# Moving two input loads from ScalarE's queue to SyncE's, so that the function table loads behind three loads, in a fused attention and rational-MLP kernel

## The chip, the cores and the metric

One core of one Trainium2 chip. The metric is device time in microseconds of one execution; most executions of one kernel here lie within 1 us of their median. Smaller is better. The span in a profile is about 1.8 us shorter than the device time of the same run.

## The reference

```python
def _attn_ref(q, k, v):                       # 8 batches, 12 heads, 448 rows, 64 columns
    scores = (1 / sqrt(64)) * q @ k^T
    m = max(scores); e = exp(scores - m)
    return (e / (sum(e) + exp(-m) + 1e-9)) @ v

def _moe_ref(x, w_in, w_out, a, b):           # x: 3584 x 768, w_in: 768 x 2048
    h = x @ w_in
    P = a[0] + a[1]*h + a[2]*h^2 + a[3]*h^3
    Q = 1 + |b[0]|*|h| + |b[1]|*h^2
    return (P / (Q + 1e-6)) @ w_out
```

The attention output, heads side by side, is x of the second part.

## The kernel before

The kernel is emitted by a small planner: operations are put into queues with estimated durations and latencies, the planner simulates the engines, and the instructions are emitted in the order it finds. Heads go in "quads" of four. For quads 0 and 1 of batch 0, float32 pieces are loaded on SyncE and ScalarE and cast to float16 by VectorE (one piece by ScalarE). Every v, and k and q from quad 2 on, are loaded by GpSimd and cast in the transfer. TensorE transposes k and q of quads 0 to 5; the head concerns 0 to 2. The exponentials are counted in the order in which ScalarE runs them; each needs its pass of scores.

```python
def first_loads():
    ...
    plan.add("c0", piece(0, 0, 0, 2, "ACT", 2.8))          # k, heads 0-1, first half
    plan.add("c0", piece(1, 0, 0, 2, "SP", 2.65))          # q, heads 0-1
    plan.add("c0", piece(0, 0, 2, 2, "ACT", 3.0, "ACT"))   # k, heads 0-1: cast by ScalarE
    piece(1, 1, 0, 2, "SP", 3.0)
    piece(0, 1, 0, 2, "ACT", 3.4)                          # k, heads 2-3
    piece(0, 1, 2, 2, "SP", 3.4)
    for pr in range(2):                                    # quad 1: k on ScalarE, q on SyncE
        for ti, (src, dst, dma) in enumerate(((k, kn, "ACT"), (q, qn, "SP"))):
            stage = quad1_stage(ti, pr)
            d = load(dma, src, 4 + 2 * pr, 2, stage, 0, J, 4.3 + 1.1 * pr)
            cast(1, ti, pr, 0, J, dst[1][:, 2 * pr:2 * pr + 2], stage, d)
    ...

# TensorE's order in the head: t* transposes (a-c, l: quad 0, d-e: quad 1, f-g: quad 2),
# s* score passes, A* sums over the exponentials and products with v
START = ("ta tb s0 tc s1 s2 td s3 s4 te s5 tf s6 s7 s9 s8 tg A0 "
         "s10 tl s11 A1 ...")

# in the main body, after first_loads():
table = plan.add("head", Op("table", "ACT", 1.3, [], lambda:
    nc.scalar.preload_act_table_set("natural_log_exp_and_others")))
...
vz = plan.add("cpt", Op("vz", "DVE", 0.06, [first_casts[0, 1, 0, 0]],
                        lambda: nc.vector.memset(vn[0][:, 0, 0, 0:2], 0.0)))
loads(0, "v")                 # GpSimd's first load; the memset before it holds it back
vload[0].deps.append(vz)
loads(2, "kq")                # quad 2
```

In the profiles, L397 is a load of `first_loads`, L402/L403 the casts, L471 the transposes, L557 the score passes, L566 the exponentials, L600 the sums and the products with v, L666 and L764 the two matrix products of the second part, L823 the function table.

The softmax here doesn't subtract the row's maximum and nothing guards it: scores larger than these inputs give would overflow.

## Time and profile before

| | kernel before |
|---|---|
| device time, median of the first 3 runs | 432.22 us (431.87 to 432.61) |
| span of the profiled run | 429.1 us (its device time 430.86 us) |
| table load | 3.74 to 5.02 us |
| first / second / seventh exponential starts | 6.43 / 8.00 / 13.46 us |
| q of quad 2 has landed | 12.69 us |
| first matmul with w_in | 27.77 us |

The profiled run was a good 1 us faster than the timed ones, so small differences of one trace to another must be held against the timed runs. The prediction below shows the lines. A line of a timeline is start, duration, engine, source line, operation, tiles, count, and in brackets the idle time before it and what ended it. A line of waits is: who waited, for whom, us in total, times, longest.

### The profile page before, as it was taken

To read this page: it belongs to the slowest core of one execution; us is meant where nothing else is said; L and a number is where in the kernel's file an instruction comes from. 1 tells how busy PE (TensorE), PEld (TensorE's weight loads), DVE (VectorE), ACT (ScalarE), POOL (GpSimd) and SP (SyncE) were. 2 spreads that over 40 slices of the span, in tenths; PEclk is the share of its full clock that TensorE was granted. 3 is DMA by queue.
4 is the path that set the end of the run, shared out by engine and by line. 5 is a ranking of instruction groups with operands and counts; after the bars stand their busy time and mean duration, and the time that the engine had idled before them with its cause. 6 is when DMAs were issued, how large, how long until landed. Compare 5 with 4: busy or idle time off the path is not lost.

```text
span 429.1 us, 8895 instructions
## 1 busy us (share of the span) xinstructions
PE 416.8 (97%) x3680; PEld 220.5 (51%) x3680; DVE 344.5 (80%) x513; ACT 328.6 (77%) x419; POOL 119.4 (28%) x170
## 2 busy tenths in 40 slices
PE   5899999999999999999999999999999999999996
PEld 3566665444444445444445544445444455555663
DVE  5344999989998869797999998789887699989500
ACT  4798999998989884988877489996788844875421
POOL 6456344365108233460013710333000000000000
PEclk9699999999999999999999999999999999999999
DMA  9999999997516994295143990296210111111222
GB/s 196 200 202 204 181 185 190 165 164 108 103 38 85 183 132 121 31 143 98 22 101 81 158 132 23 43 145 83 59 37 2 38 37 38 37 39 33 78 72 76
DMA packets 78185, 43.58 MB, mean 102 GB/s; under 512 B 36160, under 2 KB 74560, under 8 KB 78144
## 3 DMA queue, kind: packets, MB, share of 16 engines
q0 software_dynamic: 36928, 21.89, 37.5%
q1 hardware_dynamic: 39952, 20.26, 23.9%
q10 hardware_dynamic: 1264, 0.85, 0.8%
q8 instruction: 29, 0.48, 0.5%
q14 instruction: 12, 0.10, 0.1%
HBM read 45.62 MB, written 11.01 MB: 132 GB/s over the span
## 4 chain that ended last, share of the span: by engine, by line
PE 89%; DVE 5%; DMA 2%; ACT 2%; issue 1%; POOL 0%
PE gen L764 33%; PE gen L666 32%; PE gen L600 13%; PE sps L557 8%; DMA qn<-in_q_dram 2%; ACT e L566 2%; PE gen L557 1%; DVE h L683 1%; DVE n L703 1%; PE gen L471 1%; DVE n L707 1%; DMA h<-in_k_dram 1%; DVE g L707 0%; DVE c L707 0%; DVE c L703 0%
## 5 line engine op out<-in xcount | busy, mean ns | idle before, releaser
L566 ACT ACTIVATE e<-sps 112x896 f16<-112x896 f32 x156 | 137.8, 922 | 31.6 <-PE sps L557 30.9
L666 PE MATMUL gen<-x,w_in 128*128 128x448 f16 (+1 forms) x864 | 160.3, 332 | 0.0
L764 PE MATMUL gen<-w_out,g 128*128 128x384 f16 (+2 forms) x768 | 134.6, 326 | 0.7 <-DVE h L683 0.7
L666 PEld LDWEIGHTS <-w_in 128*128 128x128 f16 x864 | 80.2, 98 | 69.5 <-issue 15.7
L764 PEld LDWEIGHTS <-g 128*128 128x128 f16 x768 | 73.0, 98 | 58.6 <-issue 10.9
L683 DVE CAST h<-gen 128x448 f16<-128x448 f32 x113 | 69.3, 618 | 21.6 <-PE gen L666 17.6
L707 DVE TENSOR_TENSOR n<-n,h 128x1792 f16<-128x1792 f16 x64 | 70.2, 1096 | 1.0
L786 ACT ACTIVATE o<-gen 128x384 f32<-128x384 f32 (+2 forms) x56 | 27.9, 498 | 47.6 <-PE gen L764 46.7
L718 ACT ACTIVATE c<-c,oneeps_c 128x1792 f16<-128x1792 f16 x32 | 57.7, 1802 | 5.6 <-DVE c L707 5.5
L741 POOL COPY gx<-g 128x1024 f16<-128x1024 f16 x8 | 9.1, 1140 | 168.1 <-DVE g L707 120.5
L721 ACT ACTIVATE c<-c 128x1792 f16<-128x1792 f16 x32 | 54.8, 1713 | 0.2
L557 PE MATMUL sps<-qt,kt 64*128 64x448 f16 (+1 forms) x360 | 48.8, 341 | 2.0 <-ACT e L566 1.5
L703 DVE TENSOR_SCALAR n<-n,abc 128x1792 f16<-128x1792 f16 x64 | 44.7, 699 | 1.4
L600 PE MATMUL gen<-e,vn 112*32 112x448 f16 (+1 forms) x864 | 41.8, 337 | 0.0
L516 POOL COPY kp<-kn 112x256 uint32<-112x256 uint32 x36 | 23.0, 669 | 62.7 <-DMA kt<-kp 42.1
L628 DVE TENSOR_TENSOR x<-gen,lden 128x448 f16<-128x448 f32 (+1 forms) x54 | 28.3, 565 | 13.4 <-ACT lden L616 13.2
L707 DVE TENSOR_TENSOR g<-n,c 128x1792 f16<-128x1792 f16 x32 | 34.9, 1091 | 3.2 <-ACT c L721 2.5
L571 ACT ACTIVATE e<-gen 112x448 f16<-112x448 f32 x72 | 35.6, 560 | 0.0
L707 DVE TENSOR_TENSOR c<-c,w 128x1792 f16<-128x1792 f16 x32 | 35.0, 1092 | 0.2
L516 POOL COPY qp<-qn 112x256 uint32<-112x256 uint32 x36 | 26.9, 775 | 23.8 <-DMA qt<-qp 23.0
L557 PEld LDWEIGHTS <-kt 64*128 64x128 f16 x432 | 15.8, 96 | 32.1 <-issue 26.5
L600 PEld LDWEIGHTS <-vn 112*32 112x32 f16 x864 | 23.2, 99 | 14.1
(47 smaller groups left out, 288.9 us busy)
## 6 DMA issues: line engine op xcount, KB each, us to landing
vn<-in_v_dram POOLq DMA_DIRECT2D x24, 224.0 KB, 7.4
kn<-in_k_dram POOLq DMA_DIRECT2D x22, 224.0 KB, 7.4
qn<-in_q_dram POOLq DMA_DIRECT2D x22, 224.0 KB, 8.0
w_in<-in_moe_w_in_dram POOLq DMA_DIRECT2D x12, 256.0 KB, 9.7
w_out<-in_moe_w_out_dram POOLq DMA_DIRECT2D x4, 768.0 KB, 18.3
out_dram<-o SPq DMA_DIRECT2D x8, 336.0 KB, 3.0
out_dram<-o SPq DMA_DIRECT2D x8, 288.0 KB, 2.6
out_dram<-o SPq DMA_DIRECT2D x7, 240.0 KB, 2.5
```

Source lines behind the costliest of these rows:

```text
L516: nc.gpsimd.tensor_copy(out=mid[0].bitcast(U32)[:, pr], in_=src[n % NN].bitcast(U32)[:, 2 * pr:2 * pr + 2] .rearrange("p e j d -> p j e d"))
L557: nc.tensor.matmul(out=place(un, hh)[0:(P if i == 0 and j == 1 else 128), ci * qw:(ci + 1) * qw], lhsT=kt[n % NK][r, c0:c0 + (P if i == 0 ...
L566: nc.scalar.activation(out=e_sb[m % NE], in_=sps[un["place"][0]][0:P, :, 0:S], func=AF.Exp, scale=scale)
L571: nc.scalar.activation(out=e_sb[m % NE][:, hh], in_=gen[un["place"][hh]][0:P, 0:S], func=AF.Exp, scale=scale)
L600: nc.tensor.matmul(out=gen[unit["bank"]][32 * h:32 * h + 32, 0:qw], lhsT=lhs(h, j), rhs=e_sb[m % NE][:, h % 2, c0:c0 + qw], start=(j == 0) ...
L666: nc.tensor.matmul(out=gen[unit["bank"]][:, fi * qw:(fi + 1) * qw], lhsT=w_in_sb[wg][:, c // 2, c % 2, (fc % FG) * 128:(fc % FG + 1) * 128 ...
L683: nc.vector.tensor_copy(out=dst, in_=src)
L703: return lambda: nc.vector.tensor_scalar(out=out, in0=in0, scalar1=s1, scalar2=s2, op0=op0, **kw)
L707: return lambda: nc.vector.tensor_tensor(out=out, in0=in0, in1=in1, op=ALU.mult)
L718: lambda: nc.scalar.activation(out=c, in_=c, func=AF.Ln, bias=oneeps_c)))
L721: lambda: nc.scalar.activation(out=c, in_=c, func=AF.Exp, scale=-1.0)))
L764: nc.tensor.matmul(out=gen[unit["bank"]][:, 0:wd], lhsT=lhs, rhs=w_out_sb[f][:, fc % FG, cols], start=(fc == 0), stop=(fc == NFC - 1))
```

## The change

The intent, by its title: a third place for scores in batch 0, all quad-1 loads issued by SyncE, the function table behind three loads. The diff holds only the last two: it moves the two quad-1 k loads (quad-1 q was on SyncE before), and the table comes behind three loads by that. The new numbers at the end are the planner's estimates of latency; a comparison shows TensorE, VectorE, ScalarE and GpSimd with the same instructions in the same order. With two issues fewer on ScalarE, its table load no longer waits behind an issue that needs a used semaphore: before, it was released by the landing of the first k load and began at 3.74 us.

```diff
-            for ti, (src, dst, dma) in enumerate(((k, kn, "ACT"), (q, qn, "SP"))):
+            for ti, (src, dst) in enumerate(((k, kn), (q, qn))):
                 stage = quad1_stage(ti, pr)
-                d = load(dma, src, 4 + 2 * pr, 2, stage, 0, J, 4.3 + 1.1 * pr)
+                d = load("SP", src, 4 + 2 * pr, 2, stage, 0, J, (4.3, 3.87, 4.54, 4.11)[2 * pr + ti])
                 cast(1, ti, pr, 0, J, dst[1][:, 2 * pr:2 * pr + 2], stage, d)
```

## The prediction

> **What bounds the kernel now.** I read the busy shares on the page first, then the slices, then what TensorE waited for stretch by stretch, then the chain of waits of the first 16 us, and last the timeline of ScalarE over the first 13 us, because the change touches nothing later than 5 us.
>
> The page of the kernel before, busy time by engine and the two slice rows of TensorE and its clock:
>
> ```profile
> PE 416.8 (97%) x3680; PEld 220.5 (51%) x3680; DVE 344.5 (80%) x513; ACT 328.6 (77%) x419; POOL 119.4 (28%) x170
> ...
> PE   5899999999999999999999999999999999999996
> ...
> PEclk9699999999999999999999999999999999999999
> ```
>
> TensorE is busy in 416.8 of 429.1 us; every slice is full but the first two (10.7 us each) and the last. A change at the head can therefore win only what the head leaves idle, 12.3 us at the very most, and it wins it only if what follows can start earlier too. The view of waits, TensorE alone, from 12.7 to 31 us:
>
> ```profile
> PE sps L557 <- ACT e L566: 1.5, 4, 0.8
> PE gen L471 <- DMA qn<-in_q_dram: 0.7, 1, 0.7
> ```
>
> From 31 to 429 us the same view has only three entries, of 0.4, 0.5 and 0.2 us. So the end is the head's delay plus a nearly closed stream of TensorE work: what moves the stream at about 13 us moves the end one for one, and what moves only things before that moves nothing.
>
> The chain of work that ended last, in order of time, cut to 0 to 16 us (start, duration, what):
>
> ```profile
> 0.74 2.63 DMA h<-in_k_dram
> 3.37 0.02 issue
> 3.39 0.30 DVE kn L402
> 3.69 0.20 DVE qn L402
> 3.89 0.04 DVE vn L832
> 3.92 0.30 issue
> 4.22 0.91 POOL vn L356
> 5.13 0.69 POOL kn L356
> 5.82 6.87 DMA qn<-in_q_dram
> 12.69 0.04 issue
> 12.73 0.39 PE gen L471 x8
> 13.12 0.32 PE sps L557 x4
> 13.44 0.02 issue
> 13.46 1.73 ACT e L566 x2
> ```
>
> The reader is to see that neither the function table nor any quad-1 load is on it. It goes from the first k piece through two casts to GpSimd's loads, waits 6.87 us for the q load of quad 2, and goes on with its transposes. TensorE's order puts these transposes ahead of score pass 6, so everything behind them starts at the landing at 12.69.
>
> The timeline of ScalarE, 0 to 13 us (start, duration, instruction, idle time before it and its releaser):
>
> ```profile
> 2.22 1.49 ACTq L397 DMA_DIRECT2D g<-in_k_dram  x2
> 3.74 1.28 ACT L823 ACT_TABLE_LOAD   x1 [3.74 <-DMA h<-in_k_dram]
> 5.03 0.42 ACT L403 ACTIVATE kn<-h 112x256 f16<-112x256 f32 x1
> 6.43 0.92 ACT L566 ACTIVATE e<-sps 112x896 f16<-112x896 f32 x1 [0.98 <-PE sps L557]
> 8.00 3.47 ACT L566 ACTIVATE e<-sps 112x896 f16<-112x896 f32 x4 [0.65 <-PE sps L557]
> 11.65 0.92 ACT L566 ACTIVATE e<-sps 112x896 f16<-112x896 f32 x1 [0.18 <-PE sps L557]
> ```
>
> This is the cost that the change goes for: the second quad-1 k load needs a completion semaphore that the very first load (landed 3.37) still holds, so ScalarE's queue stood until then, and the table load behind it began at 3.74.
>
> [...] the trace has 1.28 us and shows the next ScalarE instruction right behind it (5.03), so I use the 1.28. [...] the page's slices show the DMA engines 90% busy or more from the first slice. [...] granted clock 0.50 from 14.3 to 21.1 us, after a stretch (10.9 to 14.3) in which TensorE was busy for only 1.97 of 3.40 us.
>
> **The change, part by part.** The comparison of instruction orders says that TensorE, VectorE and GpSimd keep every instruction in place. ScalarE loses two issues in front of the table load; SyncE gets them, interleaved k, q, k, q. The "third place for scores" of the title is not in the diff: the third place stays reserved for batches from 2 on, so I give it nothing.
>
> *Table load.* Three issues take ScalarE from 0.74 to 2.19 (1.45 in the row above it). The table load then runs about 2.22 to 3.50 and not 3.74 to 5.02: 1.52 us earlier. Its user, the cast of the third k piece, waits also for its data, whose last landing event I read at 4.45. So the cast starts at about 4.47 against 5.03, a gain of 0.56 us, and the first exponential at about 5.87 against 6.43.
>
> *How far that reaches.* The next passes need k and q of heads 2 and 3. Those k pieces land at 5.99 (ScalarE's third load) and 5.68 (SyncE's third), and VectorE began casting them at 6.13, 0.14 us after the landing. With the earlier cast VectorE is free at 6.0, so these casts start at about 6.02: 0.11 us of the 0.56 is left. The second exponential moves from 8.00 to about 7.89, the run of four from its end at 11.47 to about 11.36.
>
> *Then the wall.* The sixth exponential (11.65 to 12.57) may come 0.1 us earlier, but pass 6 sits behind the quad-2 q transposes, which wait for 12.69. ScalarE was already idle for 0.89 us in front of 13.46. So 0.1 us more of idle is added there, and the end moves by 0.
>
> *Loads moved to SyncE.* SyncE issues q, q, k as now (0.74 to 2.13), then quad-1 k at 2.17, q at about 2.6, then the two that wait for semaphores at about 3.4 and 3.85, where the q one now issues at about 3.2 to 3.6. The last issue is thus up to 0.6 us later, but these loads land at 7.43, 7.75, 9.23 and 9.62 by the landing events, 5.3 to 6.2 us after issue, in a queue, not at issue. In one queue they should land in order: my estimate, from some 0.34 MB per us which the packets of both queues moved together from 5 to 7.5 us and 0.23 MB a load, is 6.8, 7.5, 8.3 and 9.3 to 10.2. The quad-1 pair 0 casts stay at about 7.8 to 8.5, as now. The last cast (9.99 to 10.57 now) may slip by 0.2 us; its transposes serve pass 6, which waits until 13.05 anyway. The late q pieces, issued behind these casts, land at 15.70 and 17.93 and their transposes run at 19.5, so a slip of 0.3 us is hidden too.
>
> *The load on the path.* GpSimd's chain starts from the first k and q casts (3.39, 3.69), which the change does not touch. The bytes ahead of the quad-2 q load are the same. It lands at 12.69 again if the DMA engines are kept as full.
>
> Sum: 0.56 at the first exponential, 0.11 from the second, 0 at 12.69, so 0.0 us at the end, 432.2 us.
>
> **Rivals.** *One queue feeds the DMA engines worse.* If SyncE's single queue moved 0.25 MB per us rather than 0.34 from about 5.7 to 7.5 us, some 0.16 MB would be left over, 0.5 us at the same rate, and the q load lands at 13.2: about 432.7. For it: quad-1 loads each take over 5 us and the DMA engines are not full at 3.5 to 4.5. [...] *GpSimd's queue gets a larger share.* Its first packets came at about 7.6 while both other queues still had about 0.15 MB; [...] If a new gap of 0.3 us around 10 lost that release, eight transposes (0.39 against 0.59 at half clock) and the pass behind them would end about 0.4 us later: 432.6. [...] *The full gain reaches the end*: 0.56, or with the table's whole 1.5 us, 430.7 to 431.7. The wait at 12.69 speaks against it.
>
> **Range and chances.** The center is 432.2. The rivals reach 0.5 us down and 0.5 up, the three runs before spread by 0.4 us each way; together 431.3 to 433.1. Two per cent is 8.6 us, over two thirds of all the idle time of TensorE, and no part of the change reaches that: within 2% at 0.98.
>
> **What would show it.** Right, if in the profile after: the table load runs at about 2.2 to 3.5; the cast behind it at about 4.5; the first exponential near 5.9, but the second near 7.9; the transposes of quad-2 q start with their load's landing within 0.4 us of 12.7; the sixth exponential is followed by about 1 us of idle ScalarE. It is wrong if that landing moves by over 0.5 us, if a cast of quad 1 comes so late that pass 6 waits for it and not for quad 2, or if the half-clock stretch from 14.3 to 21.1 us changes its length or place.

The sum came to 0.56 us at the first exponential, 0.11 us from the second, 0.0 us at the end, 432.2 us. The range: its 0.5 us down is also the near end of the last rival (431.7), its 0.5 up the first (432.7). "That release" is the full clock that the trace before shows from 10.90 us; that a gap could lose it was supposition.

## The result, and the profile after

The changed kernel took 432.05 us (median of 4 runs, 431.95 to 432.33), the kernel before beside it 432.05 us (4 runs, 431.57 to 432.61). The ratio is 1.0001, 95% interval 0.9983 to 1.0018: the same. A ratio is the mean time of one kernel's fast runs over that of the other's in the same rounds, so it is not quite the ratio of the medians quoted.

ScalarE's timeline after, to be held against the one in the prediction:

```profile
2.22 1.28 ACT L823 ACT_TABLE_LOAD   x1 [2.22 <-issue]
4.18 0.42 ACT L403 ACTIVATE kn<-h 112x256 f16<-112x256 f32 x1 [0.69 <-DMA h<-in_k_dram]
5.58 0.92 ACT L566 ACTIVATE e<-sps 112x896 f16<-112x896 f32 x1 [0.98 <-PE sps L557]
7.37 1.73 ACT L566 ACTIVATE e<-sps 112x896 f16<-112x896 f32 x2 [0.87 <-PE sps L557]
9.66 1.73 ACT L566 ACTIVATE e<-sps 112x896 f16<-112x896 f32 x2 [0.57 <-PE sps L557]
11.60 0.92 ACT L566 ACTIVATE e<-sps 112x896 f16<-112x896 f32 x1 [0.21 <-PE sps L557]
13.96 0.92 ACT L566 ACTIVATE e<-sps 112x896 f16<-112x896 f32 x1 [1.44 <-PE sps L557]
```

The table load is 1.52 us earlier and the cast, the first and the second exponential follow it (0.85, 0.85 and 0.63 us earlier; part of that is a piece of data that landed earlier in this run). Most of that is gone before the seventh: the fourth exponential starts at 9.66 and not at 9.74, because its pass needs q of quad 1, which now stands behind a k load in the same queue and landed at 8.04 in place of 7.43. VectorE waited 0.47 us for it:

```profile
8.07 0.43 DVE L402 CAST qn<-g 112x512 f16<-112x512 f32 x1 [0.47 <-DMA g<-in_q_dram]
```

The sixth is only 0.05 us earlier, and in front of the seventh ScalarE now sits idle for 1.44 us where it was 0.89 us. The chain that ended last says why, 0 to 16 us, after:

```profile
5.88 6.92 DMA qn<-in_q_dram
12.80 0.04 issue
12.84 0.59 PE gen L471 x8
...
13.96 1.73 ACT e L566 x2
```

It is the same chain with the same wait of 6.9 us; the q load of quad 2 lands at 12.80 in place of 12.69. One thing differs: the eight transposes behind it took 0.59 us and not 0.39. The view of stretches shows the granted clock (the columns after the stretch and its length are the busy times of TensorE, its weight loads, VectorE, ScalarE and GpSimd with their counts, then the clock, the DMA share and GB/s). Before, then after:

```profile
10.90:14.30 3.40, 1.97 (x36) 1.15 (x33) 1.46 (x4) 2.33 (x4) 2.26 (x4) 1.00 1.43 197
14.30:17.70 3.40, 3.02 (x48) 2.08 (x51) 0.89 (x3) 2.71 (x5) 1.26 (x2) 0.50 1.37 206
```

```profile
10.90:14.30 3.40, 2.69 (x32) 1.53 (x29) 1.38 (x4) 1.75 (x3) 2.14 (x4) 1.00 1.42 198
14.30:17.70 3.40, 2.52 (x40) 1.65 (x43) 0.85 (x3) 2.75 (x4) 1.51 (x3) 1.00 1.39 206
```

The 1.00 after is misleading. The trace has clock records only from the first release on: at 10.90 us before (full until 14.32, half until 21.14, then full), at 21.69 us after. Earlier time is counted as full, but eight transposes take 0.59 us there, and 0.39 where a record says full. So in the run after, TensorE ran at half clock until 21.69 us. ("Release" below is the moment from which the records show full clock.) That left two theories for a change of nothing:

- **Wall**: what the early table gains is lost in the wait for quad-2 q, because TensorE's order puts its transposes in front of pass 6.
- **Clock**: the change gains about 0.5 us at the head and loses as much, because the early full-clock stretch is gone.

A smaller rival was that one queue feeds the DMA engines worse than two. The DMA view between 5.5 and 6.5 us answers it, before and after (queue q1 is SyncE's, q10 ScalarE's; packets, MB, share of 16 engines):

```profile
q1 hardware_dynamic: 183, 0.17, 62.8%
q10 hardware_dynamic: 164, 0.15, 49.7%
```

```profile
q1 hardware_dynamic: 345, 0.33, 108.2%
```

One queue alone moved 0.33 MB in that microsecond, two together moved 0.32; from 2.3 to 7.5 us the same view gives 1.41 MB after and 1.39 before. That rival is out.

### The profile page after: what moved, and what is told of

Same layout as the page of the kernel before. It is cut to its first block, busy times and chain, and to the rows that moved or that the text cites. A ratio compares the mean times of both kernels' runs of the same rounds, so it can differ in the third digit from the quotient of the medians.

```text
span 430.3 us, 8895 instructions
## 1 busy us (share of the span) xinstructions
PE 418.3 (97%) x3680; PEld 220.8 (51%) x3680; DVE 345.7 (80%) x513; ACT 328.7 (76%) x419; POOL 118.2 (27%) x170
## 4 chain that ended last, share of the span: by engine, by line
PE 89%; DVE 5%; DMA 2%; ACT 2%; issue 1%; POOL 0%
PE gen L764 33%; PE gen L666 32%; PE gen L600 13%; PE sps L557 8%; DMA qn<-in_q_dram 2%; ACT e L566 2%; PE gen L557 2%; DVE h L683 1%; PE gen L471 1%; DVE n L703 1%; DVE n L707 1%; DMA h<-in_k_dram 1%; DVE c L707 0%; DVE g L707 0%; DVE c L703 0%
## 5 line engine op out<-in xcount | busy, mean ns | idle before, releaser
L516 POOL COPY kp<-kn 112x256 uint32<-112x256 uint32 x36 | 25.3, 734 | 65.2 <-DMA kt<-kp 41.1
L516 POOL COPY qp<-qn 112x256 uint32<-112x256 uint32 x36 | 23.7, 687 | 23.7 <-DMA qt<-qp 21.6
```

Of the source, the lines that this page charges most:

```text
L516: nc.gpsimd.tensor_copy(out=mid[0].bitcast(U32)[:, pr], in_=src[n % NN].bitcast(U32)[:, 2 * pr:2 * pr + 2] .rearrange("p e j d -> p j e d"))
```

## The experiments

Twelve kernels ran, each timed against the kernel before on the same chip; all gave correct results. "The landing" below is that of quad-2 q.

### The changed kernel again

> The changed kernel once more, unaltered, against the kernel before in five rounds. Two theories are at stake. Wall: the earlier table load ends in the wait for the quad-2 q load (landed 12.69 before, 12.80 after), so nothing reaches the end. Clock: the earlier head is worth about 0.5 us but the changed kernel loses an early release of TensorE's clock (the profile before had full clock from 10.9 to 14.3 us, the one after had none until 21.7), worth 0.5 to 1.1 us. Wall expects a ratio of 1.000 within 0.001 and, in the trace, the landing again at 12.6 to 12.9 with ScalarE idle for over 0.9 us in front of the exponential after it. Clock expects that runs with a mean granted clock under 1.000 in the list (an early release followed by a half-clock stretch) are 0.5 to 1.1 us shorter than those at 1.000, in both kernels, and that the kernel before has more of them.

432.44 us (432.30 to 432.51, 5 runs) against 432.39 for the kernel before (431.36 to 433.23, 11 runs shared by the first four kernels): ratio 1.0002 (0.9986 to 1.0017). The landing was at 13.21 us, ScalarE idle 1.61 us in front of the seventh exponential: as the wall expects, though the landing was 0.3 us later than I wrote. The clock theory gets no support here: all five runs had a mean clock of 1.000, those of the kernel before 1.000 or 0.999. A run with the early stretch shows 0.992 (6.83 us at half of 429 us; 0.995 where that stretch is 3.41 us, as in two profiles below), so neither kernel had one in this set, and they were still equal: the loss of it is not what made the change worth nothing here. The repeat does not test the wall either, because its third piece of k landed at 6.42 us and the second exponential started at 8.10, no earlier than before the change. In the two later sets the kernel before had four such runs, 432.64, 432.26, 432.32 and 431.73 us, spread around its medians of 432.60 and 432.29. (The profiled run of the kernel before, 430.86, was one too.) The early release comes and goes, and in the kernel before it brings nothing that stands out.

### The table load alone, moved ahead of the planner

```diff
         piece(0, 1, 2, 2, "SP", 3.4)
+        casts["table"] = plan.add("head", Op("table", "ACT", 1.3, ...))   # and not after first_loads
```

> Half the change: the table load moves behind the first three loads of ScalarE, both quad-1 k loads stay on ScalarE behind it. Table load at about 2.2 to 3.5, cast behind two more issues at about 4.2 to 4.5, first exponential at 5.6 to 5.9, but quad-1 k is issued only at about 3.5 and lands at 8 or later, so the third pass of scores slips. Wall: quad-2 q still lands at 12.7 +- 0.2 and the time is that of the kernel before, ratio 0.999 to 1.001. If the table load by itself reached the end, 0.5 us would show: ratio 0.9988.

441.37 us (440.07 to 442.47), ratio 1.0207. A miss: the kernel differed in more than I had meant. Ahead of the planner the table is one of the things that it orders, and it gave another order on all engines; a comparison that ignores line numbers shows it from the first matrix product on. The waits of TensorE in this run:

```profile
PE gen L559 <- DVE x L630: 2.0, 4, 1.1
```

The full view adds 1.9 us at L668 and 0.7 at L766. In the kernel before, TensorE's waits for that tile come to 0.2 us at most. This run says nothing on the table, but a lot on how to make an experiment on a planned kernel.

### The table load alone, order kept

```diff
     plan.run()
+    at = [i for i, op in enumerate(plan.order) if op.name == "ld0ACT"][3]
+    plan.order.remove(table)
+    plan.order.insert(at, table)
     for op in plan.order:
```

> The kernel before with the table load alone moved behind the first three loads when instructions are emitted, after the planner has run, so the other orders stay as they were (the run that moved it ahead of the planner gave another order on all engines and 441.4 us). Quad-1 k is issued at about 3.6, first exponential at 5.8, second at about 8.3, fourth at about 11 because the quad-1 k load comes late, sixth at 12 to 13. Wall: ratio 0.999 to 1.001. If the 9 us of that earlier run came from the late quad-1 loads and not from the planner, this one is at about 441 too.

432.26 us (431.69 to 433.47, 6 runs) against 432.60, ratio 0.9991 (0.9979 to 1.0003): the same. So the 9 us before were the planner's order, not the late loads. The profile (its run, 433.47, was the slowest of the six) had the table at 2.22, the first exponential at 5.88, the second at 8.92 and the sixth at 13.75, later than expected. Here the late quad-1 k load (landed 9.71) was on the chain and quad-2 q (landed 13.60) was not: TensorE was still at its earlier work then. The seventh came at 15.13. So moving the table in this way has a price of its own at the head, which shows in the profile of one slow run and not in the median of six.

### One k load left in front of the table

```diff
-                d = load("SP", src, ...
+                d = load("ACT" if (ti, pr) == (0, 1) else "SP", src, ...
```

> The other half: three of the quad-1 loads on SyncE, but the second k load stays on ScalarE in front of the table load, where it waits for the first load's semaphore. Table load again at about 3.7, cast at about 5.0, first exponential at about 6.4, quad-1 landings near those of the changed kernel (7.1, 8.0 for the first two). Wall: ratio 0.999 to 1.001, quad-2 q at 12.7 +- 0.2. If moving the loads to one queue were a cost that the early table pays back, this one would be 0.3 to 0.5 us slower than the kernel before.

432.10 us (430.29 to 432.71, 6 runs), ratio 0.9991 (0.997 to 1.0013). The setup missed: as the fourth load of ScalarE in the new numbering it got a fresh semaphore and did not wait, so the table load was late by only one issue (2.72 us, first exponential 5.74). It does not part the two halves of the change; only its time, the same again, can be used.

### Three table loads in a row

In the changed kernel, the operation that loads the table loads three sets in turn (ln/exp, exp, ln/exp); every other instruction stays in place.

> The changed kernel with the function table loaded three times in a row (2.56 us more of ScalarE in front of the third piece's cast), every other instruction in its place. The cast moves from about 4.36 to about 6.1, the first exponential from 5.76 to about 7.4, the second from 8.10 to about 9.1, the sixth from 11.85 to about 12.8. Wall: that is still in front of the quad-2 q load (13.2 on that chip), so the seventh exponential stays at about 14.4 and the time at 432.4, ratio to the kernel before 0.999 to 1.001: even a table load 1 us LATER than in the kernel before costs nothing. If the table load mattered to the end, this would cost 1 to 2.5 us: 433.4 to 434.9.

432.57 us (431.83 to 432.86, 6 runs) against 432.60, ratio 0.9998 (0.9986 to 1.0009). ScalarE's timeline:

```profile
2.23 3.86 ACT L823 ACT_TABLE_LOAD   x3 [2.23 <-issue]
6.10 0.42 ACT L403 ACTIVATE kn<-h 112x256 f16<-112x256 f32 x1
...
8.84 4.37 ACT L566 ACTIVATE e<-sps 112x896 f16<-112x896 f32 x5 [0.43 <-PE sps L557]
13.94 1.72 ACT L566 ACTIVATE e<-sps 112x896 f16<-112x896 f32 x2 [0.74 <-PE sps L557]
```

This is the decisive run. The table is ready 2.6 us later than in the changed kernel and 1.07 us later than in the kernel before, the cast has moved from 4.36 to 6.10, and the exponentials up to the sixth are done at 13.21; there are still 0.74 us of idle time in front of the seventh. Nothing is lost: the interval leaves room for 0.4 us (0.0009 of 432), where 1 to 2.5 us were expected if the table mattered. The profile is one with an early release (11.04 us), so its seventh exponential may not be held against the 14.37 of the repeat; but quad-2 q landed at 13.17, and the sixth exponential was done before the transposes and pass 6 behind that landing could be. The six runs had mean clocks of 0.992 to 0.999, and the two at 0.992 (432.48 and 432.86) were not the fastest. So the table load had slack in the changed kernel, and since it was here later than in the kernel before, making it earlier only made the slack longer.

### GpSimd's first loads in another order

```diff
-                            lambda: nc.vector.memset(vn[0][:, 0, 0, 0:2], 0.0)))
-    loads(0, "v")
-    vload[0].deps.append(vz)
+                            lambda: nc.vector.memset(kn[2][:, 0, 0, 0:2], 0.0)))
     loads(2, "kq")
+    kload[2].deps.append(vz)
+    loads(0, "v")
```

> The changed kernel with GpSimd's first three loads in another order: k and q of quad 2 ahead of v of quad 0 (which is needed only at about 17 us); the memset that holds them back goes with the first one. Wall expects the landing of quad-2 q to come earlier by one load, 1.1 us (from 12.8 to about 11.7), the exponential behind it from 13.96 to about 13.0 to 13.3, and the time 0.5 to 1.0 us shorter: 431.0 to 431.5, ratio about 0.998. If the landing were not what sets the end, nothing would move.

430.68 us (429.99 to 431.84, 6 runs) against 432.39, ratio 0.9965 (0.9947 to 0.9983). The landing came at 11.96 in place of 13.21, and the seventh exponential at 13.43 in place of 14.37. Of the changed kernel run again, then of this one:

```profile
14.37 0.92 ACT L566 ACTIVATE e<-sps 112x896 f16<-112x896 f32 x1 [1.61 <-PE sps L557]
```

```profile
13.43 1.73 ACT L566 ACTIVATE e<-sps 112x896 f16<-112x896 f32 x2 [0.46 <-PE sps L557]
```

The wall moved and the end moved with it, by more than I expected (0.94 us at the seventh exponential, 1.7 us at the end by the medians). The rest goes with the clock. Both profiles were at half clock up to the first sums, which moved by the same 0.94 us (17.52 to 16.58); then the release came at 18.63 in place of 20.95, and the first matmul with w_in moved by 1.54 us (28.66 to 27.12). From that matmul to the end of the span, all profiles but those of the two kernels that the planner reordered take 401.3 to 402.3 us. The four with a remedy and no fillers, this one and three below, show the lasting release at 17.5 to 18.6 us, the six with neither at 20.7 to 22.8 (the reordered ones left out). That a head without the wait brings the release forward is the reading of these ten profiles; no run here separates the two.

### Pass 6 ahead of the quad-2 transposes

```diff
-    START = ("ta tb s0 tc s1 s2 td s3 s4 te s5 tf s6 s7 s9 s8 tg A0 "
+    START = ("ta tb s0 tc s1 s2 td s3 s4 te s5 s6 tf s7 s9 s8 tg A0 "
```

> The changed kernel with score pass 6 taken out from behind the quad-2 transposes: TensorE issues it right after pass 5. Wall: the seventh exponential follows the sixth without the wait (about 12.8 in place of 14.4), the chain then waits for quad-2 q only at passes 9 and 8, and 0.5 to 1.2 us reach the end: 431.2 to 431.9, ratio 0.997 to 0.999. If the wall is not the order behind the q load but TensorE's half clock, the seventh exponential moves and the first sums at 17.5 do not: ratio 1.000.

431.15 us (430.30 to 431.88, 6 runs) against 432.60, ratio 0.9967 (0.9954 to 0.9981). The sixth to eighth exponentials now run as one piece:

```profile
11.85 2.53 ACT L566 ACTIVATE e<-sps 112x896 f16<-112x896 f32 x3 [0.18 <-PE sps L557]
```

No load was touched here, only TensorE's order, and the gain is as large. So the wall is that order together with that load, as the wall theory has it; the first sums moved too (from 17.52 to 15.67 in the two profiles, the second with an earlier clock release, 18.04 against 20.95). The clock has a part in the size: the two runs whose mean clock (0.995 and 0.992) tells of an early release took 430.51 and 430.30 us, the other four 430.93 to 431.88.

### Both remedies, with and without the change

> The changed kernel with both remedies: quad-2 k and q ahead of v in GpSimd's queue, and pass 6 ahead of the quad-2 transposes. Each alone gave a ratio of 0.9965 and 0.9967. Wall: they take the same wait away, so together they give little more than one: ScalarE goes from the sixth to the seventh exponential without idle time, then passes 9 and 8 come at once: 430.3 to 431.2, ratio 0.994 to 0.997. If they were independent gains, 0.9932 or 429.5.

> The same two remedies in the kernel before, with its loads and its late table load. With the wait for quad-2 q gone, the run of exponentials from the second one on sets the path, and the change should now be worth what it moves the second exponential by: 0.1 to 0.6 us slower than the same kernel with the change. If that difference is again 0, the early table load is worth nothing in any of these orders because the third piece's data hold the second exponential.

With the change 430.19 us (429.76 to 430.49), ratio 0.9953 (0.9941 to 0.9965); without it 431.04 us (430.15 to 431.25), ratio 0.9970 (0.9957 to 0.9983); five runs each on one chip, the kernel before at 432.29. The means of the five are 430.15 and 430.90: 0.75 us apart, with a 95% interval of about 0.2 to 1.3 us from their spreads (0.31 and 0.43 us). With the wall gone, the kernel with the change is faster, by a little more than the 0.1 to 0.6 us that I had written. The second exponential, with and without the change:

```profile
7.16 3.56 ACT L566 ACTIVATE e<-sps 112x896 f16<-112x896 f32 x4 [0.56 <-PE sps L557]
```

```profile
8.25 3.48 ACT L566 ACTIVATE e<-sps 112x896 f16<-112x896 f32 x4 [0.64 <-PE sps L557]
```

Of these 1.09 us, 0.44 are the third piece's landing (5.44 against 5.88 us), which varies from run to run. Nor is the clock the same: the profile without the change is its fastest run, 430.15 us, the only one with an early release (mean clock 0.995); it is as fast as the mean with the change, and the other four took 431.00 to 431.25. So that the 0.75 us comes through the second exponential, and not through an earlier lasting release, is not shown. The two remedies do not add up to 0.9932. With the change, TensorE shows a new wait, which neither kernel had:

```profile
PE gen L666 <- DMA w_in<-in_moe_w_in_dram: 0.5, 1, 0.5
```

The head is now early enough to meet the next wall, the first weights of the second part.

### Fillers for TensorE's clock

> The changed kernel with 55 small idle matmuls (64x64, into unused PSUM columns) in TensorE's gaps of the first 16 us, 26 of them ahead of the first transposes. It asks what the late release of the clock is worth. Clock: the release comes at 4 to 11 us rather than 21 and holds, transposes of eight take 0.39 and not 0.59, sums of 16 take 0.57 and not 0.94; the TensorE stretch from 13.8 to 22 us shrinks, 1 to 2.5 us reach the end: 430 to 431.4. If the release does not come earlier, the fillers cost up to 0.3 us: 432.4 to 432.8.

439.98 us (438.73 to 441.00), ratio 1.0171. A miss of the same kind as before: the fillers went through the planner and 1676 rows of TensorE's order changed. Put in after the planner:

```diff
     plan.run()
+    for n, step, i in ((26, "ta", 0), (5, "s0", 0), (5, "tc", 0), (3, "td", 1),
+                       (8, "tf", 1), (6, "s9", 0), (2, "s8", 0)):
+        at = plan.order.index(steps[step][i])      # n 64x64 matmuls ahead of that operation
+        plan.order.insert(at, Op("fill", "PE", 0, [], lambda n=n: fill(n)))
```

> The 55 small matmuls again in the changed kernel, put in after the planner has run, so every engine keeps its order otherwise (the run before this one had 1676 differing rows on TensorE, and its 440 us may be those). If the fillers release the clock early and keep it: transposes of eight at 0.39, sums of 16 at 0.57, first gemm at about 27.6 and not 28.7, time 430.5 to 431.7. If the 440 us were the fillers' own doing, 438 to 441 again.

429.69 us (429.00 to 430.05, 5 runs), ratio 0.9941 (0.9927 to 0.9955): the fastest kernel, 2.6 us under the kernel before, and better than I expected. TensorE's timeline in the changed kernel, then with fillers:

```profile
12.84 0.59 PE L471 MATMUL gen<-ident,qn 112*64 112x112 f16 x8 [0.59 <-DMA qn<-in_q_dram]
...
17.11 0.94 PE L600 MATMUL gen<-e,ones 112*32 112x224 f16 x16
```

```profile
12.36 0.39 PE L473 MATMUL gen<-ident,qn 112*64 112x112 f16 x8 [0.51 <-DMA qn<-in_q_dram]
...
15.67 0.57 PE L602 MATMUL gen<-e,ones 112*32 112x224 f16 x16
```

The clock was released at 9.01 us and held. The wait for quad-2 q is still there, so this gain is in the main a different one (that load landed at 12.32 and not at 12.80 in this run, which is 0.48 us of it): behind the wall the stream is TensorE's own, and at full clock it is shorter (3.31 us from the transposes to the first sums in place of 4.27). By the first matmul with w_in the run with fillers is 2.52 us ahead (25.77 against 28.29). Less the 0.48 us, the clock is thus worth about 2 us in this head when it is held through the stretch behind the wall (an estimate from one pair of profiles). That is another thing than the short stretch from 10.9 to 14.3 us by which the first two traces differed.

### Everything together

> Both remedies and the fillers in the changed kernel: if the fillers hold the clock, another 0.5 to 1.5 us from the half-clock stretch: 429 to 430.5. If they do not, as the run with both remedies, within 0.3 us.

431.98 us (430.14 to 432.29, 6 runs), ratio 0.9988 (0.9972 to 1.0004). A miss. The fillers in front of the quad-2 transposes and passes 9 and 8 had been placed in gaps that the remedies close; here they stand in the way, at half clock, which in this run was released at 16.29 us:

```profile
13.05 0.53 PE L928 MATMUL gen<-wz 128*64 128x64 f16 x6
```

Five of the six runs show a mean clock of 0.994 to 0.996, so some stretch behind the first release was at half clock. The profiled run was the fast one of the six, at 1.000, so where that stretch lies is open. A version with both remedies and fillers placed for them was not tried.

## Why the prediction was right

- **TensorE's stream behind the head sets the end; nothing on the path is touched.** Right as to the path: the chain after is the chain before, and both remedies, which touch it, moved the end by 1.5 to 1.7 us. "One for one" was too simple: 0.94 us at 13 to 17 us became 1.54 us at the first matmul with w_in, with an earlier release of the clock.
- **Table load at 2.22 to 3.50.** Right (2.22, 1.28 us).
- **Cast at 4.47, first exponential at 5.87.** 4.18 and 5.58: the data landed at 4.16, not at 4.45. In the repeat, with the landing at 4.34, they were at 4.36 and 5.76.
- **0.11 us left at the second exponential.** It started at 7.37, and at 8.10 in the repeat: the third piece landed at 5.54 and 6.42. Counted from the landing, the exponential came 2.01 us later before, 1.83 and 1.68 us later after, so the term measures 0.18 to 0.33 us, and it lies under a landing that varies by 0.9 us. In the profile after, a wait that the prediction's sum does not count, for q of quad 1, took most of the gain before the wall.
- **Quad-1 landings 6.8, 7.5, 8.3, 9.3 to 10.2 in one queue.** 7.14, 8.04, 8.92, 9.71: in that order, 0.3 to 0.6 us later than estimated for the first three. The rate was read too high: from 5 to 7.5 us the two queues moved 0.72 MB before the change, 0.29 per us and not 0.34.
- **Landing of quad-2 q within 0.4 us of 12.7.** 12.80, and 13.21 in the repeat, which is 0.1 us outside.
- **About 1 us of idle time in front of the seventh exponential.** 1.44 and 1.61 us, partly from the transposes at half clock.
- **The half-clock stretch keeps its place.** It did not: this was named as a sign of being wrong, and in the profiled pair it moved. The sequence that the third rival supposes, no release at about 10.9 us and eight transposes at 0.59, was there (the first clock record is at 21.69). The timed runs show no cost that goes with it, and five repeats of the changed kernel were as fast as the kernel before, which had no early release in that set. That a gap in TensorE's work was what lost the release is not shown: the kernel before was busy for 3.34 of the 3.41 us up to its release at 10.90, the repeat for the same 3.34 from 7.30 to 10.71, and it had no release until 20.95; the kernel with both remedies was busy for all of 7.30 to 10.72 and released at 17.54. So the range covered this by its width; the prediction could not say which way the clock would go.
- **One queue feeds worse, or GpSimd gets a larger share.** Neither: 0.33 MB in a microsecond from one queue against 0.32 from two, and a landing of quad-2 q that did not come earlier (12.80 and 13.21 us against 12.69).

Shown: the table load has slack (three loads cost nothing), and the wait for quad-2 q in front of pass 6 is what holds the head (removing it, in two ways, gains; how much of the 1.5 to 1.7 us comes with the earlier release is open). Likely, with an interval that leaves out zero: the change is worth some 0.75 us once that wait is gone, by a path that is not shown. Only argued: that nothing of the changed kernel's zero is a small gain cancelled by a small clock loss; below 0.5 us these runs cannot tell.

## What to carry to other kernels

Before an operation at the head is made earlier, look for the next wait that everything passes, and measure the operation's slack by making it later: a doubled or tripled cost that changes nothing says more than a removed one. In a kernel with a planner, make an experiment's edit behind the planner and compare the orders first; two of twelve kernels here lost 7 to 9 us by a new order and not by what they were to test. Remedies that close the same gap did not add here (a ratio of 0.9953 for both, where 0.9932 would have been the product), and fillers made for a gap became work when the gap was gone (431.98 us with both remedies, 429.69 without).
